# V transposed as fp32 words (two bf16 rows at a time) in a one-core attention backward kernel

One core of a Trainium2 chip. The metric is the device time of one execution in microseconds (us), the median of several runs; the kernel before takes 668.1 us.

## The reference

Attention with one query per head, and its gradients: 32 heads, 8,192 keys of 128 bf16 components.

```python
def _fwd_reference(q, k, v):                      # q [1,32,1,128], k and v [1,32,8192,128], bf16
    scale = q.shape[-1] ** -0.5
    scores = jnp.einsum('bhqd,bhkd->bhqk', q, k) * scale
    attn = softmax(scores, axis=-1)
    return jnp.einsum('bhqk,bhkd->bhqd', attn, v)
# reference: out and its vector-Jacobian product with grad_out -> out, dq, dk, dv
```

For each head p = softmax(q K^T), o = p V, dp = V do, ds = p (dp - do.o) scale, dq = ds K, dK = ds q^T, dV = p do^T. K and V are read once and dK and dV written once, 2 MB each and head, 268 MB in all.

## The kernel before

A head's 8,192 keys lie as 128 partitions by 64 rows. `dp` needs V with its components along the partitions, so each 128x128 bf16 piece of V is transposed on TensorE (PE), copied out of PSUM by ScalarE (ACT), and multiplied with `do`. VectorE (DVE) does the same for K by blocks of 32, and makes dK and dV. Everything that moves is issued by one queue (SP).

```python
K_BUFS = 3; V_BUFS = 2; CH = 16                    # CH rows of 64 per chunk, 4 chunks a head
doT = consts.tile([P, H], BF16)                    # do, components along partitions
...
def v_transposes(h, c):
    T_ps = psT.tile([P, CH, P], BF16, tag="T", name="T_ps")          # 2 PSUM buffers
    for i in range(CH):
        nc.tensor.transpose(T_ps[:, i, :], Vt[h][:, c * CH + i, :], ident[:])
    X = tpool.tile([P, CH, P], BF16, tag="XT", name="XT_sb")
    nc.scalar.copy(X....bitcast(F32), T_ps....bitcast(F32))
    XV[h, c] = X

def v_scores(h, c):
    X = XV.pop((h, c))
    ...
    for i in range(CH):
        n = c * CH + i
        nc.tensor.matmul(st[h]["dp"][:, n:n + 1], lhsT=X[:, i, :], rhs=doT[:, h:h + 1], start=True, stop=True)

def contract(Xt, rep, out_col, first=0, last=NT):  # o from V and p, dq from K and ds: 64 matmuls each
    for n in range(first, last):
        nc.tensor.matmul(out_col, lhsT=Xt[:, n, :], rhs=rep[:, n, 0:1], start=(n == 0), stop=(n == NT - 1))
...
for h in range(H + 1):                             # head h, and the K gradients of head p_ = h - 1
    k_blocks, k_scores(h); load_v(h + 1)
    ds_of(p_); outer(p_, "dk", 0); dq_of(p_, 0)
    ...                                            # softmax of head h, the rest of dK and dq, load_k(h + 2)
    v_transposes(h, 0)
    contract(Vt[h], x["p"], x["m"][:, 2:3])        # o
    v_transposes(h, 1)
    ...
    v_scores(h, 0); v_transposes(h, 2); v_scores(h, 1); v_transposes(h, 3); v_scores(h, 2); v_scores(h, 3)
    outer(h, "dv", 0) ... outer(h, "dv", 3)        # dV, stored in two halves
```

## Time and profile before

| | before |
|---|---|
| time, median | 668.1 us |
| span of the profiled run | 667.0 us |
| busy: PE, weight loads, DVE, ACT | 77%, 73%, 77%, 27% |
| PE instruction pairs (load and matmul) | 10,727 |
| data moved, mean rate over the span | 268.5 MB, 403 GB/s |
| mean granted PE clock | 0.584 |

Four more of the page of the kernel before will be needed: the two groups of the V transposes (line of the source, engine, operation, out<-in, shapes, count; then busy us, mean ns of one; then idle time just before them), the dp matmuls, and the queue that fetches instructions (packets, MB, share of 16 engines).

### The profile page before, as it was taken

How to read it: one execution, taken by the hardware profiler on the slowest of the kernel's cores; microseconds unless marked ns; L12 is line 12 of the kernel's file. 1: busy time of each engine (PE TensorE's matmuls, PEld its weight loads, DVE VectorE, ACT ScalarE, POOL GpSimd, SP SyncE). 2: the span in 40 equal slices, each digit the busy share in tenths (PEclk: the TensorE clock that was granted, in tenths of full speed). 3: DMA queues.
4: the chain of work that ended last, by engine and by line, in shares of the span. 5: the costliest groups of instructions: out<-in, count | busy, mean ns of one | idle time of the engine just before them, and what ended most of it. 6: DMA issues, size and time to landing. Idle time of an engine off the chain costs nothing.

```text
span 667.0 us, 23105 instructions
## 1 busy us (share of the span) xinstructions
PE 516.8 (77%) x10727; PEld 485.8 (73%) x10727; DVE 512.5 (77%) x658; ACT 182.1 (27%) x321; POOL 0.7 (0%) x6
## 2 busy tenths in 40 slices
PE   2887988888887777878779787787776888778881
PEld 1887878878877767877668676677766777677870
DVE  4797888888877797777877778777788776887762
ACT  0333323232323222232222322223312223223230
POOL 0000000000000000000000000000000000000000
PEclk9995556566565565555555655666557665555555
DMA  8999999999999999999999999999999999999783
GB/s 330 414 425 424 419 427 414 424 423 426 425 425 424 425 425 424 425 429 423 423 427 426 423 416 422 413 412 418 395 423 418 397 416 406 409 420 403 270 357 142
DMA packets 29807, 269.94 MB, mean 405 GB/s; under 512 B 3472, under 2 KB 3472, under 8 KB 6032
## 3 DMA queue, kind: packets, MB, share of 16 engines
q1 hardware_dynamic: 29712, 268.48, 97.0%
q8 instruction: 83, 1.36, 0.7%
q14 instruction: 12, 0.10, 0.0%
HBM read 134.23 MB, written 134.23 MB: 403 GB/s over the span
## 4 chain that ended last, share of the span: by engine, by line
DMA 75%; PE 17%; DVE 3%; ACT 2%; issue 1%; SPq 0%; ACTq 0%
DMA Kt<-in_k_dram 26%; DMA Vt<-in_v_dram 26%; DMA out_dram<-G_dv 23%; PE T_ps L168 7%; PE s_ps L145 2%; PE dp_ps L185 2%; PE m_ps L185 2%; PE dp_ps L180 1%; DVE XK_sb L133 1%; ACT XT_sb L170 1%; PE m_ps L255 1%; DVE G_dk L195 1%; PE m_ps L268 1%; PE s_ps L161 0%; ACT qd L211 0%
## 5 line engine op out<-in xcount | busy, mean ns | idle before, releaser
L168 PE MATMUL T_ps<-ident,Vt 128*128 128x128 bf16 x2048 | 228.7, 302 | 31.9 <-DMA Vt<-in_v_dram 31.9
L168 PEld LDWEIGHTS <-Vt 128*128 128x128 bf16 x2048 | 201.1, 142 | 33.8 <-DMA Vt<-in_v_dram 33.6
L133 DVE STREAM_TRANSPOSE XK_sb<-Kt 128x1024 f32<-128x1024 f32 x128 | 148.2, 1213 | 81.1 <-DMA Kt<-in_k_dram 81.1
L170 ACT COPY XT_sb<-T_ps 128x1024 f32<-128x1024 f32 x128 | 129.5, 1012 | 189.7 <-PE T_ps L168 189.7
L195 DVE TENSOR_TENSOR G_dk<-ds_rep,qd 128x2048 bf16<-128x2048 bf16 x128 | 155.7, 1219 | 1.1
L195 DVE TENSOR_TENSOR G_dv<-p_rep,qd 128x2048 bf16<-128x2048 bf16 x128 | 148.2, 1220 | 8.5 <-ACT p_rep L277 8.5
L180 PEld LDWEIGHTS <-XT_sb 128*128 128x128 bf16 x2048 | 74.7, 106 | 27.2 <-ACT XT_sb L170 27.2
L180 PE MATMUL dp_ps<-doT,XT_sb 128*128 128x1 bf16 x2048 | 73.6, 166 | 24.4 <-ACT XT_sb L170 24.4
L145 PE MATMUL s_ps<-q_blk,XK_sb 128*128 128x4 bf16 x2048 | 59.1, 168 | 23.2 <-DVE pdt L216 20.5
L145 PEld LDWEIGHTS <-XK_sb 128*128 128x128 bf16 x2048 | 56.5, 103 | 25.5 <-DVE pdt L216 22.3
L185 PE MATMUL dp_ps<-ds_rep,Kt 128*128 128x1 bf16 x2048 | 64.7, 165 | 6.6 <-issue 6.0
L185 PEld LDWEIGHTS <-Kt 128*128 128x128 bf16 x2048 | 59.9, 104 | 12.3 <-issue 12.3
L185 PEld LDWEIGHTS <-Vt 128*128 128x128 bf16 x2048 | 61.1, 105 | 0.0
L185 PE MATMUL m_ps<-p_rep,Vt 128*128 128x1 bf16 x2048 | 60.5, 166 | 0.0
L226 ACT COPY dq_all<-dp_ps 128x1 f32<-128x1 f32 x32 | 5.1, 159 | 173.9 <-PE dp_ps L185 173.9
L268 PEld LDWEIGHTS m_ps<-rs,ones_f 128*128 128x128 f32 x64 | 16.0, 310 | 48.6 <-ACT e L267 48.6
L268 PE MATMUL m_ps<-rs,ones_f 128*128 128x1 f32 x64 | 18.7, 360 | 39.2 <-ACT e L267 39.2
L264 DVE TENSOR_REDUCE nbias<-m_ps 128x1 f32<-128x128 f32 x32 | 9.3, 292 | 22.0 <-ACT qd L211 22.0
L255 PE MATMUL m_ps<-diag,ones_f 128*128 128x128 f32 x64 | 25.3, 499 | 0.7 <-DVE diag L253 0.7
L218 DVE SCALAR_TENSOR_TENSOR ds_rep<-dp_ps,pdt,p_s 128x256 bf16<-128x256 f32 x32 | 15.5, 484 | 12.0 <-PE dp_ps L180 9.6
L277 ACT ACTIVATE p_rep<-e,rinv 128x256 bf16<-128x256 f32 x32 | 16.2, 507 | 30.3 <-DVE rinv L275 30.3
L211 ACT CAST qd<-m_ps 128x256 bf16<-128x256 f32 x32 | 11.9, 372 | 42.4 <-PE m_ps L207 42.4
(40 smaller groups left out, 163.0 us busy)
## 6 DMA issues: line engine op xcount, KB each, us to landing
Kt<-in_k_dram SPq DMA_DIRECT2D x31, 2048.0 KB, 28.0
out_dram<-G_dv SPq DMA_DIRECT2D x62, 1024.0 KB, 25.8
out_dram<-G_dk SPq DMA_DIRECT2D x62, 1024.0 KB, 28.0
Vt<-in_v_dram SPq DMA_DIRECT2D x30, 2048.0 KB, 28.3
Vt<-in_v_dram SPq DMA_DIRECT2D x8, 512.0 KB, 13.8
Kt<-in_k_dram SPq DMA_DIRECT2D x4, 512.0 KB, 5.4
out_dram<-G_dv SPq DMA_DIRECT2D x4, 512.0 KB, 16.9
out_dram<-G_dk SPq DMA_DIRECT2D x4, 512.0 KB, 10.7
```

The costliest lines, as they stand in the source:

```text
L133: nc.vector.transpose(XK[h][:, :, :, u, :], slots(Kt[h], u, NCH).rearrange("p g d -> p (g d)").bitcast(F32).rearrange("p (g w j) -> p g w ...
L145: nc.tensor.matmul(out[:, g, :], lhsT=cols[:, g, c // 2, c % 2], rhs=q_blk[:, h, c, :], start=(c == 0), stop=(c == 2 * NB - 1), skip_group ...
L168: nc.tensor.transpose(T_ps[:, i, :], Vt[h][:, c * CH + i, :], ident[:])
L170: nc.scalar.copy(X.rearrange("p c s -> p (c s)").bitcast(F32), T_ps.rearrange("p c s -> p (c s)").bitcast(F32))
L180: nc.tensor.matmul(st[h]["dp"][:, n:n + 1], lhsT=X[:, i, :], rhs=doT[:, h:h + 1], start=True, stop=True, skip_group_check=True)
L185: nc.tensor.matmul(out_col, lhsT=Xt[:, n, :], rhs=rep[:, n, 0:1], start=(n == 0), stop=(n == NT - 1), skip_group_check=True)
L195: nc.vector.tensor_tensor(slots(G, r, 4).rearrange("p n (a b) -> p n a b", b=R), slots(rep, r, 4).unsqueeze(2).to_broadcast([P, Q, D // R, ...
L211: nc.scalar.copy(x["qd"][:].rearrange("p a d -> p (a d)"), x["m"][:, 256:512])
L218: nc.vector.scalar_tensor_tensor(out=x["ds"][:], in0=x["dp"][:, 0:NT].unsqueeze(2).to_broadcast([P, NT, R]), scalar=pdt[:], in1=x["p_s"][: ...
L255: nc.tensor.matmul(x["m"][:, 128:256], lhsT=ones_f[:], rhs=diag[:], start=True, stop=True, skip_group_check=True)
L268: nc.tensor.matmul(x["m"][:, 0:1], lhsT=ones_f[:], rhs=rs[:], start=True, stop=True, skip_group_check=True)
L277: nc.scalar.activation(x["p"][:], e[:].unsqueeze(2).to_broadcast([P, NT, R]), ACT.Copy, scale=rinv[:])
```

## The change

Two neighbouring rows of V in a partition are 128 fp32 words, so one fp32 transpose of 128x128 words turns two bf16 rows at once. After it a partition holds a pair of components (an even and an odd one) of one of two rows. dp is then the sum of two matmuls, one over the even and one over the odd halves, against a `do` laid out in two blocks so that each row gets its own column. It halves the number of transposes and leaves the number of dp matmuls.

```diff
-    doT = consts.tile([P, H], BF16)
+    do_blk = consts.tile([P, H, 2, 2], BF16)       # zero, then filled: [word of row t, head, even/odd, t]
+    nc.vector.memset(do_blk[:], 0.0)
+    for e2 in range(2):
+        ...                                        # even (odd) components of do, twice along partitions
+        for t in range(2):
+            nc.vector.tensor_copy(do_blk[t * W:(t + 1) * W, :, e2, t], tp[t * W:(t + 1) * W, 0, 0:H])
...
     def v_transposes(h, c):
-        T_ps = psT.tile([P, CH, P], BF16, tag="T", name="T_ps")
-        for i in range(CH):
-            nc.tensor.transpose(T_ps[:, i, :], Vt[h][:, c * CH + i, :], ident[:])
+        T_ps = psT.tile([P, CH // 2, P], F32, tag="T", name="T_ps")
+        words = Vt[h].rearrange("p n d -> p (n d)").bitcast(F32)
+        for i in range(CH // 2):
+            m = c * CH // 2 + i
+            nc.tensor.transpose(T_ps[:, i, :], words[:, m * P:(m + 1) * P], ident_f[:])
...
     def v_scores(h, c):
-        for i in range(CH):
-            n = c * CH + i
-            nc.tensor.matmul(st[h]["dp"][:, n:n + 1], lhsT=X[:, i, :], rhs=doT[:, h:h + 1], start=True, stop=True)
+        for i in range(CH // 2):
+            n = c * CH + 2 * i
+            for e2 in range(2):
+                nc.tensor.matmul(st[h]["dp"][:, n:n + 2], lhsT=X[:, i, e2, :], rhs=do_blk[:, h, e2, :],
+                                 start=(e2 == 0), stop=(e2 == 1))
```

## The prediction

> **What bounds the kernel now.** I read the one-page profile first, its engine shares against its transfer row, then the chain that ended last, the windows of the middle and of the end, the timeline of one head, and the waits.
>
> The page: no engine is full, the transfers are.
>
> ```profile
> PE 516.8 (77%) x10727; PEld 485.8 (73%) x10727; DVE 512.5 (77%) x658; ACT 182.1 (27%) x321; POOL 0.7 (0%) x6
> ...
> DMA  8999999999999999999999999999999999999783
> GB/s 330 414 425 424 419 427 414 424 423 426 425 425 424 425 425 424 425 429 423 423 427 426 423 416 422 413 412 418 395 423 418 397 416 406 409 420 403 270 357 142
> ...
> q1 hardware_dynamic: 29712, 268.48, 97.0%
> ```
>
> 268.5 MB must move whatever the engines do. At 424 GB/s that is 633 us of the 667, so only some 34 us lie in the slices at the two ends. The chain that ended last says the same: three quarters of it is DMA, and the V transposes, the group that the change rewrites, are its largest compute link with 7%.
>
> ```profile
> DMA 75%; PE 17%; DVE 3%; ACT 2%; issue 1%; SPq 0%; ACTq 0%
> ```
>
> Its order in time matters more than its shares. Until 132 us it runs through PE, with a head every 17.1 to 20.3 us (the starts of the K score matmuls: 30.3, 47.4, 67.7, 84.8, 103.9, 122.0). From 132 to 626.5 us it is DMA only: a V load, a K load and a store of dV, some 27 us each, three of them (82 us) for every four heads. From 626.5 us, when the last K has landed, it is compute again. But DMA is full in the first stretch too: the windows give 419 GB/s and a share of 1.01 from 20 to 615 us, and 259 GB/s from 615 to 667. A shorter PE chain before 615 us can therefore only make PE wait longer.
>
> The slack shows in the timeline of a middle head, with the wait in brackets:
>
> ```profile
> 328.96 1.89 PE L168 MATMUL T_ps<-ident,Vt 128*128 128x128 bf16 x16 [1.55 <-DMA Vt<-in_v_dram]
> ...
> 332.39 1.87 PE L168 MATMUL T_ps<-ident,Vt 128*128 128x128 bf16 x16
> ...
> 336.40 4.62 DVE L133 STREAM_TRANSPOSE XK_sb<-Kt 128x1024 f32<-128x1024 f32 x4 [3.52 <-DMA Kt<-in_k_dram]
> ...
> 342.35 0.34 SPq L81 DMA_DIRECT2D Vt<-in_v_dram  x1
> ```
>
> A head takes 20.57 us here (K scores at 320.51 and 341.08), of which PE is busy 16.57. PE waits 1.55 us for V, DVE 3.52 us for K. The last transposes of this head stop reading V at about 338.6 us, but the load that wants this buffer is issued at 342.35, so 3.7 us lie there too.
>
> **What the Trainium skill says.** "TensorE: Matmul & The Clock Gate", Part 4: PE-mode transpose, gives about 275 ns for a bf16 transpose in a kernel. The trace has 302 ns as the mean duration, but they pipeline: 16 take 1.73 us in the chain, 108 ns each. The same page, LDWEIGHTS, has weights load at 1.2 columns per ns (107 ns for 128), and Weight-path perf modes has a fast weight load for 128 columns that is not for fp32. The trace agrees: 64 bf16 loads with tiny matmuls take 1.70 us, 27 ns each, while the two fp32 loads of one matmul start 170 to 215 ns apart. Third, the Terms of that page give the transpose mode as "4× faster for FP32". No trace here has an fp32 transpose, so this is the open figure of the case. Fourth, "DMA: Bandwidth & Descriptors", Where 436 GB/s comes from, puts a fabric ceiling at 435 GB/s; the trace's 424 is 97% of it, so I expect no faster DMA.
>
> **The change part by part.** Call X the time PE needs for one of the four V chunks' transposes (now 16 x 108 ns = 1.73 us).
>
> 1. V transposes: 2,048 in bf16 become 1,024 in fp32. The compiled program of the changed kernel has 9,705 weight loads and as many matmuls against 10,727 now: 2,048 fewer, 1,024 more and 2 in the setup. So an fp32 transpose is one load and one matmul, not the two of each that an ordinary fp32 matmul has here (64 records for 32). What one costs I bracket: if the load hides behind the stream of 128 columns, 107 ns, X = 0.86 us. If the fp32 load (about 200 ns) sets the pace, X = 1.6. If the pair runs like one pass of the fp32 128-column matmul, whose two matmuls start 340 ns apart, X = 2.7. I take 200 ns, X = 1.6: half the count at nearly twice the price.
> 2. ScalarE's copy of a chunk: the same 128x1024 fp32 words, 1.01 us, 128 times, nothing changes. The two PSUM buffers hold the same 4 KB per partition.
> 3. dp: still 2,048 matmuls, now with two columns (one row's products, the other zero) and weights read with a stride of two elements, accumulating in pairs. The K scores already do this with four columns and the same stride: 103 ns load, 168 ns matmul against 106 and 166 for dp now. No cost.
> 4. Setup: on DVE two copies of rows, a memset and four half copies come and one copy goes, about 7 x 0.17 - 0.17 = 1.0 us (from the 0.14 to 0.21 us of the like operations in the first 12 us), with two small PE transposes at 0.2 us between them: up to 1.5 us ahead of the first K scores. DMA has 10 MB queued by then (24 us at 424 GB/s), so most of it is hidden.
>
> Where it counts: before 615 us not at all as long as PE keeps inside 20.4 us a head (the mean from 122 to 631). PE's own chain is 17.1 to 18.2 us where it waits least, of which 6.9 are transposes. At X = 1.6 it becomes 16.6 to 17.7. In the tail the four chunks of the last head lie on the end's path, uncovered: 4 x (1.73 - X) = 0.5 us gained at X = 1.6, 3.5 at X = 0.86. With some tenths of the setup against it the sum is 668.1 - 0.5 + 0.4, rounded with the slight risk upward: 667.5.
>
> **The rivals.** (a) Transposes at 107 ns. For it: one matmul record each, the skill's "4×", and that bf16 loads hide wholly now. It halves the largest PE group, about 110 us of work, but only the tail shows it, and there ScalarE's 1.01 us copies become the pace with two PSUM buffers. Time 664 to 666. (b) PE becomes the bound. For it: in the fp32 matmuls the load visibly doesn't hide (passes of 128 columns start 340 ns apart, passes of one column 180 to 210). At X = 2.7 a head's chain grows by 3.9 us to 21 to 22 us, beyond the 20.4 of DMA: some 31 x 1.1 us plus 4 us in the tail, 695 to 705. Its threshold is X of about 2.5, 310 ns a transpose: then the 3.1 us added still fit, barely, into the V wait, the DVE wait and the 3.7 us before the next V load. Against it: the second pass is what transposes don't have. (c) A faster PE frees V sooner, loads start sooner, and transfers collide differently. At 424 GB/s there is nothing to gain, and the queue of SP mostly waits for earlier transfers to land (the V load waits 55.8 us in total for dV stores, 22.2 for the transposes). Within 2 us of now. (d) DMA moves faster because PE or PSUM traffic falls: nothing in the profile links them, and the rate sits at its ceiling.
>
> **How the range and the chances follow.** (a) and the central case give 664 to 668; run scatter is 0.7 us. So the low end is 662. The high end must cover mild forms of (b), X up to 2.6: 686. I give X above 2.5 one chance in six. Faster by over 2% needs 13 us, which the exposed 3.5 us can't give: 0.01.
>
> **What would show it.** In the changed profile the fp32 transpose group should have 1,024 records; the start spacing within a chunk of 8 gives X directly. If I am right the middle stays at 415 to 425 GB/s, the chain stays DMA between about 132 and 626 us, PE's busy time falls, and its waits for V and for DVE grow by what X saves. The dp group should keep 27 ns spacing. The tail from the last K landing to the end should shrink by 4 x (1.73 - X). I am wrong if the middle's rate falls below some 410 GB/s with PE full and the chain turning to transposes (X over 2.5), or if dp's strided pairs stall.

## More of the kernel before

```profile
q8 instruction: 83, 1.36, 0.7%
...
L168 PE MATMUL T_ps<-ident,Vt 128*128 128x128 bf16 x2048 | 228.7, 302 | 31.9 <-DMA Vt<-in_v_dram 31.9
L168 PEld LDWEIGHTS <-Vt 128*128 128x128 bf16 x2048 | 201.1, 142 | 33.8 <-DMA Vt<-in_v_dram 33.6
...
L180 PE MATMUL dp_ps<-doT,XT_sb 128*128 128x1 bf16 x2048 | 73.6, 166 | 24.4 <-ACT XT_sb L170 24.4
```

The transposes are PE's largest group. The queue of instructions moves 1.36 MB in the whole run, half a percent of what the data queue moves.

## The result, and the profile after

663.9 us (663.1 to 664.0, 4 runs) against 668.1 (667.5 to 668.9, 4 runs): ratio 0.9933, 95% interval 0.9916 to 0.9951. A ratio here is the mean time of one kernel's fast runs over that of the other's of the same rounds, so it is not quite the ratio of the medians quoted. The verdict is "same" by the 2% rule, and 4.2 us (0.7%) faster beyond doubt.

The page of the changed kernel, the lines that answer to those shown of before:

```profile
PE 505.4 (76%) x9705; PEld 470.8 (71%) x9705; DVE 513.4 (78%) x664; ACT 182.4 (28%) x321; POOL 0.7 (0%) x6
...
q1 hardware_dynamic: 29712, 268.48, 97.1%
q8 instruction: 76, 1.25, 0.7%
...
DMA 70%; PE 21%; DVE 3%; ACT 2%; issue 1%; SPq 0%; ACTq 0%
...
L180 PE MATMUL T_ps<-ident_f,Vt 128*128 128x128 f32 x1024 | 222.6, 390 | 30.9 <-DMA Vt<-in_v_dram 30.8
L180 PEld LDWEIGHTS T_ps<-ident_f,Vt 128*128 128x128 f32 x1024 | 183.9, 208 | 32.1 <-issue 30.0
...
L192 PE MATMUL dp_ps<-do_blk,XT_sb 128*128 128x2 bf16 x2048 | 71.6, 164 | 24.7 <-ACT XT_sb L182 24.7
```

Half as many transposes, and nearly the same busy time (222.6 for 228.7 us): an fp32 transpose costs what two bf16 ones cost. dp is as dear as before (164 for 166 ns). So PE won almost nothing where the change meant it to.

Pieces of the chain that ended last show it without the overlap (start, us, what): first the kernel before, a chunk at the full PE clock (granted clock 1.00), the first DVE work on the last head's K, and a chunk at the low clock (0.50), then the same of the changed kernel.

```profile
44.76 0.93 PE T_ps L168 x16
...
626.50 4.62 DVE XK_sb L133 x4
...
638.08 1.73 PE T_ps L168 x16
```

```profile
157.72 0.95 PE T_ps L180 x8
...
621.89 4.63 DVE XK_sb L142 x4
...
633.39 1.81 PE T_ps L180 x8
```

A chunk takes 1.81 us where it took 1.73 (226 ns a transpose for 2 x 108), or 0.95 for 0.93 when the clock is up. But the last K has landed at 621.9 instead of 626.5 us, 4.6 us earlier, and from there to the end both kernels take as long: 667.0 - 626.5 = 40.5 and 662.2 - 621.9 = 40.3 us. The whole gain lies ahead of the last K, in the stretch that is bound by transfers. The windows of 20 to 600 us (busy time and count of PE, weight loads, DVE, ACT, POOL; granted clock; DMA share; GB/s), before and after:

```profile
20.00:600.00 580.00, 466.20 (x9719) 438.73 (x9718) 463.14 (x582) 163.84 (x290) 0.00 (x0) 0.58 1.01 419
```

```profile
20.00:600.00 580.00, 458.97 (x8881) 428.72 (x8880) 465.58 (x585) 165.96 (x294) 0.00 (x0) 0.60 1.01 422
```

The share is 1.01 both times, yet the same transfers go 0.7% faster. What made full DMA engines faster?

**The sixteen landings.** Each transfer of 128 partitions runs on 16 DMA engines, and each adds one to the transfer's semaphore when its part has landed; the trace holds these sixteen times. I took them for all transfers that landed from 100 to 600 us, sorted each set, and took the median distance from the last (us):

```
before  -17.5 -17.4 -17.3 -17.3 -17.3 -16.4 -15.0 -10.4 -10.2 -10.1  -9.5  -9.1  -8.7  -8.5  -8.1   0
after   -15.5 -15.5 -15.4 -15.4 -15.4 -14.4 -12.9  -9.0  -8.7  -8.6  -8.4  -8.2  -8.1  -7.5  -6.3   0
```

In the median, fifteen engines are done 6 to 17 us ahead of a sixteenth, and with the change it lags less. (The lag builds up along the run: in the changed kernel the last landing is 0.7 us behind the second last around 120 us and 10.3 around 560.) The transfers use eight semaphores in turn, so at most eight are in flight, and a new one starts only when an old one has landed on *all* engines: the sixteenth sets the pace. The mean share of 1.01 hides it, because the others' packets are in flight meanwhile.

**Theory** (fetch): the sixteenth engine also fetches the instructions. A PE instruction has 64 bytes (the compiled PE program shrank by 131,072 bytes for the 2,048 instructions that the half dose below drops), so 10,727 pairs are 1.37 MB, besides some 0.1 MB for the other engines. By the theory that engine carries, per head, 512 KiB, 524.3 KB, of data and 42.9 KB of PE's instructions, 567.2 KB; with the change (1,244,992 bytes of PE program, over 32) 563.2 KB. The ratio, 0.9929, is what was measured (0.9933). This is what I planned the runs by. They bear out that instructions cost time; that the sixteenth engine fetches them is contradicted by the packets of the same traces, which are read further down. **Rivals**: PE time, that is, the head's chain through PE got shorter somewhere; fewer PSUM writes or SBUF reads by PE that disturb transfers less; chance of scheduling.

### The profile page after: what moved, and what is told of

It is laid out like the page before. It is cut to its first block, busy times and chain, and to the rows that moved or that the text cites. A ratio compares the mean times of both kernels' runs of the same rounds, so it can differ in the third digit from the quotient of the medians.

```text
span 662.2 us, 21100 instructions
## 1 busy us (share of the span) xinstructions
PE 505.4 (76%) x9705; PEld 470.8 (71%) x9705; DVE 513.4 (78%) x664; ACT 182.4 (28%) x321; POOL 0.7 (0%) x6
## 2 busy tenths in 40 slices
DMA packets 29800, 269.83 MB, mean 407 GB/s; under 512 B 3472, under 2 KB 3472, under 8 KB 6032
## 4 chain that ended last, share of the span: by engine, by line
DMA 70%; PE 21%; DVE 3%; ACT 2%; issue 1%; SPq 0%; ACTq 0%
DMA Kt<-in_k_dram 26%; DMA Vt<-in_v_dram 25%; DMA out_dram<-G_dv 19%; PE T_ps L180 9%; PE s_ps L154 2%; PE m_ps L197 2%; PE dp_ps L197 2%; PE dp_ps L192 2%; ACT XT_sb L182 1%; DVE XK_sb L142 1%; PE m_ps L267 1%; PE m_ps L280 1%; DVE G_dk L207 1%; ACT e L279 1%; ACT qd L223 1%
## 5 line engine op out<-in xcount | busy, mean ns | idle before, releaser
L180 PE MATMUL T_ps<-ident_f,Vt 128*128 128x128 f32 x1024 | 222.6, 390 | 30.9 <-DMA Vt<-in_v_dram 30.8
L180 PEld LDWEIGHTS T_ps<-ident_f,Vt 128*128 128x128 f32 x1024 | 183.9, 208 | 32.1 <-issue 30.0
L142 DVE STREAM_TRANSPOSE XK_sb<-Kt 128x1024 f32<-128x1024 f32 x128 | 148.1, 1213 | 72.4 <-DMA Kt<-in_k_dram 72.3
L192 PEld LDWEIGHTS <-XT_sb 128*128 128x128 bf16 x2048 | 73.3, 103 | 29.5 <-ACT XT_sb L182 27.5
L192 PE MATMUL dp_ps<-do_blk,XT_sb 128*128 128x2 bf16 x2048 | 71.6, 164 | 24.7 <-ACT XT_sb L182 24.7
L197 PEld LDWEIGHTS <-Vt 128*128 128x128 bf16 x2048 | 62.5, 105 | 2.0
## 6 DMA issues: line engine op xcount, KB each, us to landing
out_dram<-G_dk SPq DMA_DIRECT2D x4, 512.0 KB, 10.3
```

The lines of the kernel that those rows point to most:

```text
L142: nc.vector.transpose(XK[h][:, :, :, u, :], slots(Kt[h], u, NCH).rearrange("p g d -> p (g d)").bitcast(F32).rearrange("p (g w j) -> p g w ...
L180: nc.tensor.transpose(T_ps[:, i, :], words[:, m * P:(m + 1) * P], ident_f[:])
L192: nc.tensor.matmul(st[h]["dp"][:, n:n + 2], lhsT=X[:, i, e2, :], rhs=do_blk[:, h, e2, :], start=(e2 == 0), stop=(e2 == 1), skip_group_chec ...
```

## The experiments

Twelve runs. All times are medians of fast runs (e9: one run, state unknown) beside the kernel before on the same chip, whose median was 667.7 to 668.1 us each time. MB is what both instruction queues fetched. The lag is that of the last landing behind the second last, median over the transfers issued from 150 to 560 us; in this window it is 9.1 us before and 7.2 after.

| run | what | MB | us | ratio to before | lag us |
|---|---|---|---|---|---|
| before | | 1.46 | 668.1 | 1 | 9.1 |
| after | | 1.35 | 663.9 | 0.9933 | 7.2 |
| e1 | after + 2,046 idle weight loads | 1.48 | 706.1 | 1.058 | 0.5 |
| e2 | after + 2,046 tiny GpSimd instructions | 1.48 | 667.4 | 0.9996 | 9.9 |
| e12 | after + 217 longer GpSimd instructions | 1.36 | 663.8 | 0.9937 | 7.6 |
| e3 | after - 2,048 PE instructions | 1.21 | 659.9 | 0.9882 | 6.1 |
| e7 | after - 4,096 PE instructions | 1.08 | 657.8 | 0.9848 | 5.8 |
| e8 | before - 2,048 PE instructions | 1.35 | 663.6 | 0.9942 | 7.3 |
| e5 | after + 1,023 idle pairs | 1.48 | 665.4 | 0.9960 | 7.1 |
| e6 | after, same count, longer o matmuls | 1.35 | 662.8 | 0.9921 | 6.7 |
| e4 | after, 8 K loads in two | 1.35 | 716.6 | 1.074 | |
| e9 | after, 7 K loads in three | | 697.2 (one run) | | |
| e10 | after, 5 dV stores on 15 + 4 engines | | 721.4 | 1.080 | |
| e11 | after, 5 dK stores on 15 + 4 engines | | 712.7 | 1.064 | |

### e1: more PE instructions, first try

```diff
+        if h < H - 1:
+            for _ in range(66):
+                nc.tensor.ldweights(ident[:])
         v_transposes(h, 0)
```

> The changed kernel with 66 idle weight loads of the identity ahead of each head's V transposes (not the last head), where PE waits for V anyway: 2,046 PE instructions more, about as many as the change took away, 131 KB of instructions. Fetch theory (the 16 data engines are not alike: in the traces 15 of them finish a transfer 6 to 8 us before the last one, and the last is the one that also fetches PE's instructions, 64 bytes each; a head costs what that engine carries): its bytes per head go from 563.2 to 567.3 KB, so the time goes back by 0.7%, to about 668, ratio to the kernel before 1.000. Rival, PE time or scheduling: the 1.8 us a head lie in PE's wait for V, so the time stays at 664, ratio 0.993. In the trace the last data engine's lag grows again by some 1.8 us under the first theory only.

706.1 us, outside both. The loads were no cheap ballast: in the timeline of e1 66 of them take 3.33 us, 50 ns each, where a load with a one-column matmul behind it takes 27.

```profile
319.57 3.33 PEld L294 LDWEIGHTS <-ident 128*128 128x128 bf16 x66
...
322.84 1.97 PE L180 MATMUL T_ps<-ident_f,Vt 128*128 128x128 f32 x8 [2.92 <-PE L294]
```

The transposes now wait for PE's own loads and no longer for V: PE is the bound. The lag falls to 0.5 us, presumably because transfers that are issued late let every engine catch up. The run says nothing on the theory, but it shows the PE slack that the prediction estimated: 3.3 us a head more cost some 42 us over 31 heads, 1.4 a head, so about 2 us were free.

### e2 and e12: instructions of another engine, and its control

```diff
# e2                                                       # e12
+            nc.gpsimd.tensor_copy(idle[:], x["p_s"][0:1, 0:1])   # the same, idle of 1,024 words
+            for _ in range(65):                           # range(6)
+                nc.gpsimd.memset(idle[:], 0.0)            # one word: 89 ns   (1,024 words: 942 ns)
         v_transposes(h, 0)
```

> The changed kernel with 66 tiny instructions a head on the idle GpSimd (2,046 in all, 133 KB of instructions), PE's program untouched. Fetch theory in its narrow form (only what shares the DMA engine of PE's fetches counts): GpSimd's fetches are on another ring, and if that lies on another engine, no change, ratio 0.993 to 0.994. Fetch theory in its wide form (any fetched byte counts, or the rings share an engine): 668, ratio 1.000. Plain bandwidth (0.13 MB at 424 GB/s): 0.3 us, ratio 0.994.

> The control to the 2,046 tiny GpSimd instructions: the changed kernel with one copy and six longer writes of 1,024 words a head on GpSimd, so about as much busy time of GpSimd (some 5 us a head, estimated) and more bytes written to SBUF, but 217 instructions instead of 2,046 (16 KB fetched instead of 133). Fetch theory: no change, 664, ratio 0.993 to 0.994. If the tiny instructions had cost time through GpSimd's use of SBUF beside DVE: 667 or more, ratio 0.999 or above.

e2 took back the whole gain: 0.9996, with the PE program untouched. e12 has the same busy time of GpSimd and took back none: 0.9937 (interval 0.9923 to 0.9950). The pages, first of e2, then of e12 (engine busy; then packets, MB and share of the instruction queues):

```profile
PE 524.0 (79%) x9705; PEld 488.3 (73%) x9705; DVE 513.5 (77%) x664; ACT 182.2 (27%) x321; POOL 185.3 (28%) x2052
...
q8 instruction: 76, 1.25, 0.7%
q14 instruction: 28, 0.23, 0.1%
```

```profile
PE 521.2 (79%) x9705; PEld 486.3 (73%) x9705; DVE 513.6 (78%) x664; ACT 182.3 (28%) x321; POOL 181.4 (27%) x223
...
q8 instruction: 76, 1.25, 0.7%
q14 instruction: 14, 0.11, 0.0%
```

DVE's busy time is the same in both, so GpSimd's use of SBUF isn't what costs. What differs is 1,829 instructions (0.12 MB on queue 14), and the lag: 9.9 against 7.6 us. So the time is that of the theory's wide form: GpSimd's instructions cost about what PE's do, and the last engine's lag grows with them. (Its reason, a shared engine for the fetches, is not so; see the packets below.) Plain bandwidth would give 0.3 us; 3.6 were measured. This pair also rules out PE time and PE's memory traffic as the only cause.

### e3 and e7: fewer PE instructions

```diff
# e3 and e7 (wrong on purpose: dp from the even components)
-            for e2 in range(2):
+            for e2 in range(1):
# e7 and e8 (wrong on purpose: o from every second row)
-        contract(Vt[h], x["p"], x["m"][:, 2:3])
+        for n in range(0, NT, 2):
+            nc.tensor.matmul(x["m"][:, 2:3], lhsT=Vt[h][:, n, :], rhs=x["p"][:, n, 0:1],
+                             start=(n == 0), stop=(n == NT - 2))
```

> The changed kernel without the second of the two dp matmuls (wrong on purpose: dp from the even components alone): 2,048 PE instructions fewer, 131 KB. Fetch theory: 563.2 to 559.1 KB a head, 0.7% less, about 659.5, ratio to the kernel before 0.986 to 0.987. Rival (PE has slack before 615 us and the change gained by chance of scheduling): only 4 x 0.4 us of dp in the tail, 663 to 664, ratio 0.992 to 0.993.

> A double dose the other way (wrong on purpose): the changed kernel without the second dp matmul and with every second o matmul left out, 4,096 PE instructions and 262 KB fewer. Fetch theory, 4.0 us for each 131 KB as the single dose gave: 656, ratio 0.982. If instead the single dose only used up some last slack: 659 to 660, ratio 0.988. The tail may give 0.8 us of its own.

e3: 659.9 us, 0.9882; the fetch theory had 0.986 to 0.987, the rival 0.992 to 0.993. e7: 657.8, 0.9848, between the 0.982 of a straight line and the 0.988 of a gain used up. The first 131 KB fewer gave 4.0 us, the next 2.1: the return falls off. Outputs are wrong.

### e8: the kernel before with the changed kernel's instruction count

> The kernel before, all bf16, with every second o matmul left out (wrong on purpose): 19,416 PE instructions less those waiting, as many as the changed kernel to within 40. Fetch theory: what the change gained was its count of instructions, not its fp32 transposes, so this has the changed kernel's time: 663 to 664.5, ratio 0.993 to 0.994. If the gain came from fewer PSUM writes or fewer transposes: 667 to 668, ratio 0.998 to 1.000, less 0.85 us of the tail.

663.6 us, 0.9942 (0.9929 to 0.9954): all bf16, twice the transposes, and the changed kernel's time. Its PE program has 1,242,624 bytes, the changed one's 1,244,992. This is the plainest evidence that the gain is not that of fp32 transposes but that of 2,044 instructions fewer. Half of the o matmuls are also 0.85 us of PE time a head, so it doesn't by itself exclude PE time; e2 with e12 does.

### e5 and e6: PE time and instruction count apart

```diff
# e5
+            for _ in range(33):
+                nc.tensor.matmul(x["m"][:, 3:4], lhsT=ident[:], rhs=ident[:, 0:1], start=True, stop=True)
         v_transposes(h, 0)
# e6: 49 of 64 o matmuls stream 64 columns, all but the first into unused PSUM
+            w = 64 if h < H - 1 and 4 * n + 64 <= 4 * NT else 1
+            nc.tensor.matmul(x["m"][:, 2:2 + w], lhsT=Vt[h][:, n, :], rhs=flat[:, 4 * n:4 * n + w], ...)
```

> The first idle weight loads took 50 ns each and made PE the bound, so the dose is given again in a cheaper form: the changed kernel with 33 idle pairs of load and one-column matmul (27 ns a pair, 0.9 us a head) ahead of each head's V transposes, 2,046 PE instructions and 131 KB more. Fetch theory: 567.3 KB a head on the last data engine as in the kernel before, 668, ratio 1.000, and its lag behind the second last back from 7 to 9 us. PE-time theory: 0.9 us are inside PE's slack of some 2 us, 664, ratio 0.993.

> The counterpart: the changed kernel with the same number of PE instructions, but more PE time: 49 of the 64 matmuls of o stream 64 columns instead of one (extra columns to unused PSUM, result unchanged), some 26 ns each, 1.3 us a head, last head excepted. Fetch theory: no change, 664, ratio 0.993 to 0.994. PE-time theory: at least as slow as the idle pairs, 668 or more.

e6 came out at 662.8 us, not slower than the changed kernel (0.9921 against 0.9933; the intervals overlap), as the fetch theory expected and the PE-time theory did not. Its transposes became cheaper, as its groups show:

```profile
L180 PE MATMUL T_ps<-ident_f,Vt 128*128 128x128 f32 x1024 | 168.6, 319 | 35.4 <-DMA Vt<-in_v_dram 35.4
```

168.6 us for the changed kernel's 222.6, at a mean granted clock of 0.681 instead of 0.611: the longer streams kept the clock up, so total PE time wasn't raised (486.6 us busy for 505.4) and the run is no test of PE time. It has the lowest time of a correct kernel, 1.1 us below the changed kernel.

e5 is a miss: 0.9960 where 1.000 was expected, so 1.5 us lost of the 4.2, and the lag (7.1) didn't grow. The fetched bytes are there (1.48 MB), and the time theory's 0.993 lies outside its interval (0.9947 to 0.9972) too. Charged for all its instructions, its last engine moved more bytes per us than in any other run (below). Why is open; by the packets below that engine's stores are as in the changed kernel and only its loads longer.

### A number that should be constant

If the last engine is always busy and fetches the instructions, its data plus these over the time is its rate, the same in every kernel. From the landings and the fetch packets between the first and the last big transfer issued from 150 to 570 us (data / 16 alone, then with all fetched bytes; GB/s):

```
            before  after   e2     e12    e3     e7     e8     e6     e5
data / 16   25.34   25.55  25.40  25.57  25.75  25.84  25.50  25.64  25.54
with fetch  27.54   27.60  27.66  27.66  27.64  27.52  27.53  27.69  27.87
```

The first row follows the times; the second is constant within 0.6% but for e5. One packet of 16 KB at the window's edge is 0.04. This is a fit and no proof: it charges each instruction 64 bytes, and doesn't show that they are fetched by this engine.

**The packets, against the theory.** The traces also list each DMA packet with its start, length and queue. On one engine a packet begins where the one before ended, and every engine serves the same sequence of packet sizes, so the list can be strung into sixteen chains. (They hold to about 450 us; later the leading engines pause, and the chains can't be told apart.) From 130 to 450 us one chain is the last in all 92 transfers of the changed kernel, in 91 of 91 before, and in at least 86 of 91 in each other run of the table. This chain carries none of PE's fetches: the 337 fetch packets of the nine runs in this span, 16 KB each, take turns on eight other chains. Nine of GpSimd's in e2 lie on a ninth. The last chain has a single fetch of 8 KB. So the last engine is not the one that fetches.

What makes it last is the length of its own packets. An 8 KB packet of a store takes 309 ns at best. On the last chain of the changed kernel it took 312 ns on average when no PE instruction ended meanwhile and 376 when 24 or more did: 2.3 ns for each load or matmul. In e2 each GpSimd instruction added 2.6 ns (standard error 0.5). On the other fifteen chains these packets took 309 to 312 ns, whatever PE did. What its store and load packets (611 ns at best) took beyond the best, summed from 40 to 450 us, nearly follows the times of the runs; store and load are not equally affected, and why loads differ isn't known (in e5 the stores are as in the changed kernel, 18.1 for 17.8 us, and the loads not, 3.2 for 1.5):

```
            before  after   e2     e12    e3     e7     e8     e6     e5
excess, us  21.8    19.3   22.3   19.1   17.1   15.9   21.1   18.3   21.3
```

So instructions that run slow this one engine's stores, and the fetched bytes were only another count of them. What each instruction sends that way the traces don't show. A rival stands untested: every timed run comes with a span and a granted clock from its trace, so the records that the profiler keeps of each instruction may be what costs. No run without them is there.

### e4 and e9: which engine is it?

```diff
# e4, in load_k                                            # e9
-            nc.sync.dma_start(t, r)
+            for a, b in ((0, 120), (120, P)) if h % 4 == 3 else ((0, P),):     # (0,112,112+n,P), n = 2 to 8
+                nc.sync.dma_start(t[a:b], r[a:b])
```

> The changed kernel with every fourth K load (8 of 32) as two transfers, 120 partitions and 8: by the skill the first is spread over 15 DMA engines and the second over 8. If the engine that also fetches instructions is not among those used, it is relieved of 8 x 128 KB, 33 of its 563 KB a head, and the time falls by up to 5.8% of the 600 us between the ends, to 628 to 640, ratio 0.94 to 0.96. If it is among them, nothing or 0.5% slower, 664 to 667. A theory of plain bandwidth says no gain: the same bytes, 8 transfers more.

The Trainium skill, "DMA: Bandwidth & Descriptors", Why a DMA increments its semaphore by 16 and not by 1, has a transfer run on the largest number of engines up to 16 that divides the slowest dimension: 15 for 120 partitions, 8 for 8. The trace agrees: packets under 512 bytes rose from 3,472 to 3,528, and 8 x (15 + 8 - 16) = 56.

716.6 us, 7% slower. In all eight split loads the late landing is in both parts, so the last engine is among the 15 and among the 8: no relief. The split also hurts by itself: the load issued at 374.2 us has its last landing at 408.1, 34 us later instead of 28, and DVE waits 7.15 us for that K instead of 3.3. That the eight splits together cost 53 us is not accounted for in full.

> A look only, to find out which data engine is the last one. The changed kernel with seven of the K loads cut in three by partitions: 112 rows (16 engines, 7 rows each), n rows and 16 - n rows, with n = 2 to 8. By the skill a transfer of n rows runs on n engines. If these are always the first n of the sixteen, the late landing (7 us and more after the others) is missing in the pieces of n rows up to the place of the last engine and there in those above it; the run with 15 and 8 of 16 had it in all of both, so its place is among the first eight. If the late landing is in every piece down to 2 rows it is the first or second engine, and no such split can relieve it. Time: slower than the changed kernel, as the split in two was (more, smaller transfers in the same eight places), 700 to 730.

Landings of the pieces of two heads (us; the last value of a row is the late engine's, where it is in the set):

```
112 rows  ... 258.2 259.2 259.3 261.0 261.0 261.1 261.5 263.1      (16 engines)
  4 rows  253.6 255.4 255.8 256.4                                  late landing absent
 12 rows  ... 260.4 260.5 261.7 262.8 263.2 264.4
112 rows  ... 341.7 344.2 344.5 346.3 347.2 347.5 347.5 351.6
  5 rows  338.1 339.4 341.3 341.5 352.4                            late landing present
 11 rows  ... 347.5 348.6 348.6 353.0
```

It is absent for 3 and 4 rows and present for 5, 6, 7 and 8. (It is absent for 2 as well, but so early in the run that the 112 rows show no lag either.) If n rows run on the first n engines, the last one is the fifth. This is one execution. The skill's same page, Latency and other measured facts, calls engines 7 and 15 usually slower; here neither stands out as this one does.

### e10 and e11: passing the fifth engine by

```diff
+        if which == "dv" and h in (4, 10, 16, 22, 28):    # e11: "dk"
+            if r == 3:
+                for lo, hi in ((68, P), (0, 68)):          # 60 rows on 15 engines, 68 on 4
+                    nc.sync.dma_start(rows_of(dst, h, 0, 1)[lo:hi], G[lo:hi])
+            return
```

> The look at subsets put the late landing in the pieces of 5 rows and more and not in those of 2, 3 and 4: the last engine is the fifth, and transfers of 4 engines pass it by. The changed kernel where in heads 4, 10, 16, 22 and 28 the two column halves of the dV store become two row parts, 60 rows (15 engines, 4 rows each) and 68 rows (4 engines, 17 rows each): as many transfers as before, same bytes. The fifth engine moves 64 KB less in each, 0.32 MB of its 18 in all, the first four 0.21 MB more each, 7.8 us of theirs, about the lead they have. Fetch theory: up to 0.32 MB at 27.6 GB/s, 11.6 us; with some lost to transfers that start later, 652 to 660, ratio 0.977 to 0.988. Plain bandwidth: 664 or slower, ratio 0.993 or above.

> The same with the dK stores of these heads, where the first half is then issued some 5 us later in its head. Fetch theory: the same relief, 652 to 662, ratio 0.977 to 0.991, rather the upper part. Plain bandwidth: 664 or slower.

Both failed: 721.4 and 712.7 us. (e11's profiled run was slow; its time and ratio are from its three fast runs.) Between two splits of e10 a head takes 19.5 us (V loads issued at 149.1, 168.6, 188.2 and 207.7) where the changed kernel takes some 20.4, so the last engine was relieved. But the four that took its share became the late ones: after the split at 224.7 us the last four landings of the next V load come 16 to 30 us after the median one. My sum was wrong in two ways. I counted on the four engines' lead each time, as if it grew back between splits; and 1.06 MB more on each (17.8 MB, at the 26.9 GB/s between the splits, 512 KiB in 19.5 us) is 663 us, no better than the changed kernel. They also fell back by 12 to 16 us in this split instead of 7.8; why isn't settled. No version that moves the share was found.

## Why the prediction was right or wrong

1. **The bound** (transfers, with slack on PE and DVE ahead of the last K): right. The chain is DMA from 159 to 622 us, and e1 puts the PE slack at about 2 us a head.
2. **One transpose at 200 ns, X = 1.6 us**: the right bracket and nearly the size. Measured 226 ns and 1.81 us at the low clock. "Half the count at nearly twice the price" became a little more than twice. Rivals (a) at 107 ns and (b) at 340 ns both fell.
3. **The tail**: 0.5 us were to be gained; with X = 1.81 it is 4 x (1.73 - 1.81) = -0.3 of the transposes, and measured from the last K the tails are 40.5 and 40.3 us. So the only place in which I looked for a gain gave none worth naming. The prediction's sum was also wrong as written: 668.1 - 0.5 + 0.4 is 668.0 and not 667.5, so its terms give a gain of 0.1 us. Rival (b)'s terms, 31 x 1.1 + 4 on top of 668.1, give 706, just outside its 695 to 705.
4. **dp at no cost**: right, 164 ns for 166.
5. **Setup, up to 1.5 us, mostly hidden**: right. The first K scores start at 13.05 instead of 12.37 us, and the first two slices move 335 and 410 GB/s instead of 330 and 414.
6. **"I expect no faster DMA" and rival (d), "nothing in the profile links them, and the rate sits at its ceiling"**: this step failed, and it holds the whole gain, 4.2 us where 0.6 was predicted. The 424 GB/s are a sum over sixteen engines; the pace is set by one whose stores take longer the more instructions run. The count stood in the page and in my own working (10,727 pairs to 9,705, 2,044 instructions): charged at 64 bytes on one engine of 27.6 GB/s they are 4.7 us. Rival (c) came near in asking for a freed transfer, but looked for it in V's buffer.
7. **The waits for V and DVE would grow by what X saves**: wrong. X saved nothing, and DVE's wait for K fell from 81.1 to 72.3 us in total.

The time lay in the range and the direction was right by luck: the reason was not in the prediction. Shown by e2 with e12, and in line with e3 and e8: the number of instructions costs time in these traced runs, whichever engine runs them. Shown by the packets: one DMA engine is last, it fetches next to nothing (one packet of 8 KB from 130 to 450 us), and its stores lengthen with the instructions that run. Open: what each instruction sends there, whether an execution that isn't traced has it, e5's half effect, and the falling return in e7.

## What to carry to other kernels

When a kernel is bound by transfers and unrolled into tens of thousands of instructions, count its instructions: here, in traced runs, 1,000 PE instructions cost about 2 us. Try it without the profiler before building on it. Look at the landings of a transfer engine by engine before calling DMA full; a mean share of 1.0 can hide one late engine. And judge a change that trades instructions for dearer instructions by its count too: here the intended saving on PE was nil and the count gave the gain. And a sum that comes out constant is not yet a mechanism: the packet list, at hand from the start, showed that the fetches lie elsewhere.

## What the Trainium skill lacked or had wrong

- No page has a cost of running instructions for transfers: 2,046 tiny GpSimd instructions took 3.5 us (e2), where 217 longer ones took none (e12), and on one of sixteen engines 8 KB store packets went from 312 to 376 ns with the PE instructions that ended meanwhile. Nor does one say which DMA engines fetch: here PE's 16 KB fetches take turns on eight.
- "DMA: Bandwidth & Descriptors", Latency and other measured facts, names engines 7 and 15 as the slower ones; in this kernel it is the fifth by one look (e9), 7 to 9 us behind the others.
- The same page gives the rule for the number of engines, which the packets confirm (56 more in e4), and advises to use all 16, without a cost: five stores with 68 rows on 4 engines cost over 50 us (e10).
- "TensorE: Matmul & The Clock Gate" has "4× faster for FP32" and no time for an fp32 transpose: 226 ns back to back at the low clock and 119 at the high one, against 108 and 58 for bf16 here. By words moved that is no gain over two bf16 transposes.
